# GroupNorm on one core: per-engine programs with hand-set semaphores, loops on TensorE and VectorE, all channels scaled on VectorE, 64 KB store rows

## The chip, the cores and the metric

The kernel runs on one core of one Trainium2 chip. The metric is the device time of one execution in microseconds. The kernel before takes 633.61 us (median of 3 runs, 633.52 to 633.78).

A core has five engines that run their own instruction streams: TensorE (PE), VectorE (DVE), ScalarE (ACT), GpSimd (POOL) and SyncE (SP), which issues the DMAs here. Sixteen DMA engines move data between HBM and the on-chip memory SBUF, whose 128 partitions are the rows that all engines work on; TensorE writes its results to PSUM.

## The reference

A GroupNorm over `x` of shape (128, 1024, 32, 16) in bf16: 128 samples, 32 groups of 32 channels, 512 pixels per channel. For each sample and group the mean and the variance are taken over 32 x 512 = 16384 elements.

```python
xr = x.reshape(B, G, C // G, H, W)
mu = xr.mean(axis=(2, 3, 4), keepdims=True)
var = ((xr - mu) ** 2).mean(axis=(2, 3, 4), keepdims=True)
xn = (xr - mu) / jnp.sqrt(var + 1e-5)
xn = xn.reshape(B, C, H, W)
return xn * g[None, :, None, None] + b[None, :, None, None]
```

The input is 134.2 MB and the output as large, so 268.4 MB pass the DMA engines.

## The kernel before

The work is cut into 32 tiles of 128 partitions. A partition holds one group of one sample: 32 channels of 512 elements, 32 KB in bf16, so a tile is 4 MB; here a tile `i` is called a unit. In tile `i` the partitions are 4 samples by 32 groups, and the 4 MB lie in one piece in HBM. Six tiles `xt` fit into SBUF at a time (`XBUFS`), and everything happens in place in them.

For each unit, in this order:

- `L(i)` (line 101) loads it through SP's queue; the first and the last unit are loaded in quarters, the others in one DMA of 4 MB.
- `M(i)` (line 166) sums over the free dimension: 32 matmuls with the identity `eye` as weights add the 32 slices of 512 columns into one PSUM tile `pa`. Each matmul has its own weight load.
- `R0(i)` (line 189): VectorE multiplies the PSUM tile by -1/16384 and accumulates it into `negmean`.
- `Q(i)` (line 244): ScalarE computes Square(x + negmean) over each half of the unit (128 x 8192) and accumulates the sum.
- `V(i)` (lines 308 to 353): ScalarE takes the square root of the variance, VectorE the reciprocal `rstd`, GpSimd the 32 factors per channel `scl`, `shift` and `bia`.
- `A(i)` (lines 363 and 368): each channel is scaled by `x * scl + bia`. Of the 32 channels VectorE does 16, GpSimd 13 and ScalarE 3.
- `S(i)` (line 381): the unit is stored, the last two units in quarters.

The main loop starts the sum of unit i+1 (`M`, `R0`) ahead of `V(i)` and `A(i)`, and `finish(i-1)`, which holds ScalarE's three channels, the store and the next loads, stands inside `Q(i)` between the two squares. The loads after the first six are issued in pairs, when two units have been stored; a load waits on SP until the store of the unit that had the buffer has landed. A tile framework writes the semaphores; `chain` only fixes the order of instructions on each engine. Units 0 and 31 are `shifted`: their squares are taken around the mean of their first quarter.

Of the kernel before, what the change touches and what calls it, by code (L numbers as in the profile page):

```python
# [9 lines left out]
ALU = mybir.AluOpType  # L10
F32 = mybir.dt.float32
# [6 lines left out]
XBUFS = 6  # L18
UPFRONT = 6
RUN = 2  # L20
MM_FREE = 512
QUARTERS = 4
STORE_IN_PARTS = 2
ACT_SHARE = 2
LAST_SHARE = 3
POOL_SHARE = 13
# [3 lines left out]
def kernel(  # L30
# [7 lines left out]

# [5 lines left out]
    assert P % G == 0 and C % G == 0  # L49
    NS = P // G  # L50
    assert B0 % NS == 0
    NT = B0 // NS
# [3 lines left out]
    MMN = MM_FREE  # L56
    NMM = F // MMN
    NQ = QUARTERS
    QF = F // NQ
    KQ = KC // NQ  # L60
    MQ = NMM // NQ
    assert NQ == 4 and F % (NQ * MMN) == 0 and KC % NQ == 0

    x_v = x.rearrange("(t n) (g k) h w -> t (n g) (k h w)", n=NS, g=G)
    o_v = out.rearrange("(t n) (g k) h w -> t (n g) (k h w)", n=NS, g=G)
    g_v = g.rearrange("(g k) -> g k", g=G)
    b_v = b.rearrange("(g k) -> g k", g=G)

    consts = ctx.enter_context(tc.tile_pool(name="consts", bufs=1))
    xpool = ctx.enter_context(tc.tile_pool(name="xpool", bufs=XBUFS))  # L70
    jpool = ctx.enter_context(tc.tile_pool(name="jpool", bufs=1))
    spool = ctx.enter_context(tc.tile_pool(name="spool", bufs=4))
    pspool = ctx.enter_context(
        tc.tile_pool(name="pspool", bufs=2, space=bass.MemoryType.PSUM)
    )
    gpool = ctx.enter_context(
        tc.tile_pool(name="gpool", bufs=1, space=bass.MemoryType.PSUM)
    )

    last = {}  # L80
    nosync = mybir.DependencyInfo(
        mybir.DependencyClass.NoSync, mybir.DependencyReason.DATA
    )

    def chain(key, inst):
        prev = last.get(key)
        if prev is not None:
            tc.add_manual_dep(inst.ins, prev.ins.name, nosync, reason="pipeline order")
        last[key] = inst
        return inst  # L90

    state = {}

    def L(i):
        xt = xpool.tile([P, F], BF16, name="xt")
        parts = NQ if i == 0 or i >= NT - 1 else 1
        w = F // parts
        for c in range(parts):
            chain(
                "sp",  # L100
                nc.sync.dma_start(  # L101
                    out=xt[:, c * w : (c + 1) * w], in_=x_v[i][:, c * w : (c + 1) * w]
                ),
            )
        state[i] = {"xt": xt}

    for i in range(min(UPFRONT, NT)):
        L(i)

    gb_b = consts.tile([G, 2, KC], BF16)  # L110
    chain("act", nc.scalar.dma_start(out=gb_b[:, 0, :], in_=g_v))
    chain("act", nc.scalar.dma_start(out=gb_b[:, 1, :], in_=b_v))
    eps_t = consts.tile([P, 1], F32)
    nc.vector.memset(eps_t[:], EPS)
    warm = consts.tile([P, 1], F32)
    chain("act", nc.scalar.activation(out=warm[:], in_=eps_t[:], func=ACT.Sqrt))  # L116

    ones_b = consts.tile([P, P], BF16)
    nc.vector.memset(ones_b[:], 1.0)
    eye = consts.tile([P, P], BF16)  # L120
    nc.gpsimd.affine_select(
        out=eye[:],
        in_=ones_b[:],
        pattern=[[-1, P]],
        compare_op=ALU.is_equal,
        fill=0.0,
        base=0,
        channel_multiplier=1,
    )
    rep = consts.tile([G, P], BF16)  # L130
    nc.gpsimd.affine_select(
        out=rep[:].rearrange("q (n a) -> q n a", n=NS),
        in_=ones_b[0:G, :].rearrange("q (n a) -> q n a", n=NS),
        pattern=[[0, NS], [-1, G]],
        compare_op=ALU.is_equal,
        fill=0.0,
        base=0,
        channel_multiplier=1,
    )
    gb = consts.tile([P, 2, KC], F32)  # L140
    gam = gb[:, 0, :]
    bet = gb[:, 1, :]

    def GB():
        gb_p = gpool.tile([P, 2, KC], F32, name="gb_p")
        chain(
            "pe",
            nc.tensor.matmul(  # L148
                out=gb_p[:].rearrange("p a k -> p (a k)"),
                lhsT=rep[:],  # L150
                rhs=gb_b[:].rearrange("q a k -> q (a k)"),
                start=True,
                stop=True,
            ),
        )
        chain("dve", nc.vector.tensor_copy(out=gb[:], in_=gb_p[:]))  # L156

    def shifted(i):
        return i == 0 or i == NT - 1

    def matmuls(st, name, lo, hi):
        ps = pspool.tile([P, MMN], F32, name=name)
        for k in range(lo, hi):
            chain(
                "pe",
                nc.tensor.matmul(  # L166
                    out=ps[:],
                    lhsT=eye[:],
                    rhs=st["xt"][:, k * MMN : (k + 1) * MMN],
                    start=(k == lo),  # L170
                    stop=(k == hi - 1),
                ),
            )
        st[name] = ps

    def M(i):
        st = state[i]
        if shifted(i):
            matmuls(st, "pa", 0, MQ)
            matmuls(st, "pb", MQ, NMM)  # L180
        else:
            matmuls(st, "pa", 0, NMM)

    def sum_of(ps, seed, name):
        total = spool.tile([P, 1], F32, name=name)
        jd = jpool.tile([P, MMN], BF16, name="jd")
        chain(
            "dve",
            nc.vector.tensor_scalar(  # L189
                out=jd[:],  # L190
                in0=ps[:],
                scalar1=-inv_n,
                scalar2=seed,
                op0=ALU.mult,
                op1=ALU.add,
                accum_out=total[:],
            ),
        )
        return total

    def R0(i):
        st = state[i]
        if shifted(i):
            st["q"] = sum_of(st["pa"], None, "q")
        else:
            st["negmean"] = sum_of(st["pa"], None, "negmean")

    def R1(i):
        st = state[i]
        if not shifted(i):  # L210
            return
        st["negmean"] = sum_of(st["pb"], st["q"][:], "negmean")
        off = spool.tile([P, 1], F32, name="off")
        chain(
            "pool",
            nc.gpsimd.tensor_scalar(  # L216
                out=off[:],
                in0=st["negmean"][:],
                scalar1=1.0 / NQ,
                scalar2=st["q"][:],  # L220
                op0=ALU.mult,
                op1=ALU.subtract,
            ),
        )
        seed = spool.tile([P, 1], F32, name="seed")
        chain(
            "pool",
            nc.gpsimd.tensor_scalar(
                out=seed[:],
                in0=off[:],  # L230
                scalar1=-1.0,
                scalar2=off[:],
                op0=ALU.mult,
                op1=ALU.mult,
            ),
        )
        st["seed"] = seed

    def squares(st, w, k, bias, scale, sq):

        ja = jpool.tile([P, F // 2], FP8, name="ja")
        chain(
            "act",
            nc.scalar.activation(  # L244
                out=ja[:, 0:w],
                in_=st["xt"][:, k * w : (k + 1) * w],
                func=ACT.Square,
                bias=bias,
                scale=scale,
                accum_out=sq,  # L250
                saturate=False,
            ),
        )

    def Q(i):

        st = state[i]
        if shifted(i):
            sq = spool.tile([P, NQ], F32, name="sq")
            for k in range(NQ):  # L260
                squares(st, QF, k, st["q"][:], 1.0 / NQ, sq[:, k : k + 1])
                if k == 0:
                    finish(i - 1)
            st["sq"] = sq
            return
        s0 = spool.tile([P, 1], F32, name="s0")
        s1 = spool.tile([P, 1], F32, name="s1")
        squares(st, F // 2, 0, st["negmean"][:], 1.0, s0[:])
        v0 = spool.tile([P, 1], F32, name="v0")
        finish(i - 1)  # L270
        chain(
            "pool",
            nc.gpsimd.tensor_scalar(  # L273
                out=v0[:],
                in0=s0[:],
                scalar1=inv_n,
                scalar2=EPS,
                op0=ALU.mult,
                op1=ALU.add,
            ),  # L280
        )
        squares(st, F // 2, 1, st["negmean"][:], 1.0, s1[:])
        st["v0"], st["s1"] = v0, s1
# [177 lines left out]
```

## Time and profile before

| what | value |
|---|---|
| device time, median of 3 runs | 633.61 us |
| the profiled execution: span of the profile | 632.5 us |
| DMA: share of the span that the data queue q1 kept 16 engines busy | 99.0% |
| HBM traffic over the span | 424 GB/s |
| busy: PE, DVE, ACT, POOL | 260.9, 379.0, 537.9, 345.3 us |
| squares on ACT, each 128 x 8192 | 7109 ns, 60 of them |
| scaling one channel: DVE, POOL, ACT (means) | 730, 801, 799 ns |
| one matmul of 128 x 512 (mean) | 421 ns |

The profile is of one execution, whose span lies 1.1 us below the median of the runs; its own device time is not listed, so 632.5 + 1.1 us is used for it. The page gives busy times per engine, a strip of 40 slices of the span, the DMA queues and groups of instructions by line; a timeline lists instructions with their start and duration; a list of waits says who waited for whom.

### The profile page before, as it was taken

The page shows a single profiled execution, that of the slowest core. Times are in us where ns is not written, and L with a number is a line of the kernel's source. Part 1 is how long each engine was busy: PE and PEld are TensorE (multiplying, and loading weights), DVE is VectorE, ACT ScalarE, POOL GpSimd, SP SyncE. Part 2 cuts the span into 40 slices and gives each one's busy share as a digit, 9 for nine tenths or more (in the row PEclk, how much of TensorE's full clock was granted, in tenths as well). Part 3 has the DMA queues.
Part 4 walks back from the last instruction along what each step waited for, and adds up shares of the span by engine and source line. Part 5 has one row for each costly group of instructions (what it writes and reads, how often), then busy time and mean ns, then how long its engine had stood idle before and what let it go on. Part 6 is the DMA issues. An engine that isn't in the chain of part 4 may idle for free.

```text
span 632.5 us, 3907 instructions
## 1 busy us (share of the span) xinstructions
PE 260.9 (41%) x1025; PEld 106.4 (17%) x1025; DVE 379.0 (60%) x645; ACT 537.9 (85%) x268; POOL 345.3 (55%) x523
## 2 busy tenths in 40 slices
PE   5577609064180632806327063270723607146000
PEld 2223203021030210302113021030301203012000
DVE  1077766666676477563665636666466663657660
ACT  4599999999999699696996969969798796987960
POOL 0077776666666377563665636666365663657100
PEclk9789759668595675957759577595875958758555
DMA  9999999999999999999999999999999999999996
GB/s 371 437 428 406 436 433 431 433 429 433 429 424 433 429 437 431 432 434 433 434 432 424 432 433 431 429 432 432 431 431 431 436 429 432 431 425 435 431 423 260
DMA packets 11063, 268.70 MB, mean 425 GB/s; under 512 B 1312, under 2 KB 1312, under 8 KB 1312
## 3 DMA queue, kind: packets, MB, share of 16 engines
q1 hardware_dynamic: 10944, 268.44, 99.0%
q8 instruction: 8, 0.13, 0.1%
q14 instruction: 15, 0.12, 0.0%
q10 hardware_dynamic: 96, 0.00, 0.0%
HBM read 134.22 MB, written 134.22 MB: 424 GB/s over the span
## 4 chain that ended last, share of the span: by engine, by line
DMA 62%; ACT 15%; PE 9%; issue 5%; DVE 3%; POOL 2%; SPq 0%; DVEq 0%; ACTq 0%; POOLq 0%
DMA out_dram<-xt 40%; DMA xt<-in_x_dram 21%; ACT ja L244 13%; PE pa L166 9%; DVE xt L368 3%; ACT xt L363 2%; POOL xt L368 1%; DMA gb_b<-in_g_dram 0%; ACT rstd L308 0%; POOL scl L337 0%; POOL shift L343 0%; POOL bia L353 0%; SPq L101 0%; DVE rstd L312 0%; DVE jd L189 0%
## 5 line engine op out<-in xcount | busy, mean ns | idle before, releaser
L244 ACT ACTIVATE ja<-xt,negmean 128x8192 fp8e5<-128x8192 bf16 x60 | 426.6, 7109 | 55.2 <-DVE jd L189 55.1
L166 PE MATMUL pa<-xt,eye 128*128 128x512 bf16 x976 | 250.1, 421 | 317.9 <-DMA xt<-in_x_dram 317.9
L368 DVE TENSOR_SCALAR xt<-xt,scl,bia 128x512 bf16<-128x512 bf16 x536 | 351.4, 730 | 39.8 <-POOL bia L353 39.8
L368 POOL TENSOR_SCALAR xt<-xt,scl,bia 128x512 bf16<-128x512 bf16 x390 | 307.5, 801 | 3.4 <-POOL bia L353 0.3
L166 PEld LDWEIGHTS <-eye 128*128 128x128 bf16 x1024 | 106.3, 106 | 472.2 <-DMA xt<-in_x_dram 318.8
L337 POOL TENSOR_SCALAR scl<-gb,rstd 128x32 f32<-128x32 f32 x31 | 11.1, 358 | 220.1 <-DVE rstd L312 220.1
L189 DVE TENSOR_SCALAR_CACHE_REDUCE jd<-pa 128x512 bf16<-128x512 f32 x32 | 21.9, 684 | 113.9 <-PE pa L166 113.9
L363 ACT ACTIVATE xt<-xt,bia,scl 128x512 bf16<-128x512 bf16 x98 | 72.0, 799 | 0.8 <-DVE bia L324 0.8
L312 DVE RECIPROCAL rstd<-rstd 128x1 f32<-128x1 f32 x32 | 5.2, 163 | 72.7 <-ACT rstd L308 72.7
L244 ACT ACTIVATE ja<-xt,q 128x4096 fp8e5<-128x4096 bf16 x8 | 29.7, 3706 | 6.6 <-DVE jd L189 6.4
L343 POOL TENSOR_SCALAR shift<-scl,negmean 128x32 f32<-128x32 f32 x31 | 11.1, 358 | 3.1
L216 POOL TENSOR_SCALAR off<-negmean,q 128x1 f32<-128x1 f32 x2 | 0.9, 430 | 20.4 <-DVE jd L189 20.4
L166 PE MATMUL pb<-xt,eye 128*128 128x512 bf16 x48 | 11.0, 379 | 0.6 <-DMA xt<-in_x_dram 0.6
L244 ACT ACTIVATION_READ_ACCUMULATOR ja<-xt,negmean 128x1 f32 x60 | 11.2, 187 | 0.0
L308 ACT ACTIVATE rstd<-s,v 128x1 f32<-128x1 f32 x30 | 8.8, 294 | 2.8
L353 POOL TENSOR_TENSOR bia<-shift,gb 128x32 f32<-128x32 f32 x31 | 7.8, 251 | 2.6
L273 POOL TENSOR_SCALAR v<-s 128x1 f32<-128x1 f32 x30 | 5.7, 191 | 2.5
L308 ACT ACTIVATE rstd<-var,eps_t 128x1 f32<-128x1 f32 x2 | 0.6, 294 | 7.5 <-DVE jv L292 7.5
L156 DVE COPY gb<-gb_p 128x64 f32<-128x64 f32 x1 | 0.2, 225 | 5.5 <-PE gb_p L148 5.5
L116 ACT ACT_TABLE_LOAD x1 | 1.3, 1283 | 1.7 <-PEq L445 1.7
L189 DVE DVE_READ_ACCUMULATOR jd<-pa 128x1 f32 x32 | 2.6, 80 | 0.0
L292 DVE TENSOR_SCALAR_CACHE_REDUCE jv<-sq,seed 128x4 f32<-128x4 f32 x2 | 0.4, 214 | 2.7 <-ACT ja L244 2.7
(18 smaller groups left out, 6.1 us busy)
## 6 DMA issues: line engine op xcount, KB each, us to landing
xt<-in_x_dram SPq DMA_DIRECT2D x30, 4096.0 KB, 19.4
out_dram<-xt SPq DMA_DIRECT2D x30, 4096.0 KB, 29.3
xt<-in_x_dram SPq DMA_DIRECT2D x8, 1024.0 KB, 11.5
out_dram<-xt SPq DMA_DIRECT2D x8, 1024.0 KB, 17.9
gb_b<-in_g_dram ACTq DMA_DIRECT2D x1, 2.0 KB, 3.2
gb_b<-in_b_dram ACTq DMA_DIRECT2D x1, 2.0 KB, 5.2
```

The source lines that it names most:

```text
L116: chain("act", nc.scalar.activation(out=warm[:], in_=eps_t[:], func=ACT.Sqrt))
L166: nc.tensor.matmul(out=ps[:], lhsT=eye[:], rhs=st["xt"][:, k * MMN : (k + 1) * MMN], start=(k == lo), stop=(k == hi - 1),),
L189: nc.vector.tensor_scalar(out=jd[:], in0=ps[:], scalar1=-inv_n, scalar2=seed, op0=ALU.mult, op1=ALU.add, accum_out=total[:],),
L244: nc.scalar.activation(out=ja[:, 0:w], in_=st["xt"][:, k * w : (k + 1) * w], func=ACT.Square, bias=bias, scale=scale, accum_out=sq, satura ...
L273: nc.gpsimd.tensor_scalar(out=v0[:], in0=s0[:], scalar1=inv_n, scalar2=EPS, op0=ALU.mult, op1=ALU.add,),
L308: nc.scalar.activation(out=rstd[:], in_=last_sum[:], func=ACT.Sqrt, bias=bias[:], scale=scale),
L312: chain("dve", nc.vector.reciprocal(out=rstd[:], in_=rstd[:]))
L337: nc.gpsimd.tensor_scalar(out=scl[:], in0=gam, scalar1=rstd[:], scalar2=None, op0=ALU.mult),
L343: nc.gpsimd.tensor_scalar(out=shift[:], in0=scl[:], scalar1=st["negmean"][:], scalar2=None, op0=ALU.mult,),
L353: nc.gpsimd.tensor_tensor(out=bia[:], in0=shift[:], in1=bet, op=ALU.add),
L363: inst = nc.scalar.activation(out=span, in_=span, func=ACT.Identity, bias=bia, scale=scl)
L368: inst = eng.tensor_scalar(out=span, in0=span, scalar1=scl, scalar2=bia, op0=ALU.mult, op1=ALU.add,)
```

## The change

The work per element is the same. What differs:

- **Layout.** A partition row in HBM is now 64 KB: two neighbouring groups of one sample. 8 samples by 16 pairs of groups make 128 rows, and each of the 32 units is one half (32 KB) of all rows, so that a unit's load takes 32 KB out of every 64 KB. The six buffers lie side by side in one tensor `ring`, so that two neighbouring units can be stored as one DMA of 128 rows of 64 KB (8 MB).
- **Order of DMAs.** All on SP, written by hand: six loads; then units 0 to 5 stored one by one with loads between; units 6 to 29 stored in 12 pairs, each pair followed by two loads; unit 30 alone; unit 31 in four parts. In the steady part the first of the two loads needs the pair stored before, the second one the pair just issued.
- **TensorE** loads the identity once and issues the matmuls without a weight load; a loop of 5 rounds with 6 units in each.
- **ScalarE** does the squares, one small ACTIVATE that forms `part`, and the root; no channels. Each of its steps waits for its own step before.
- **VectorE** loops over 31 units: reciprocal, `scl`, `bia`, the mean of the next unit, then all 32 channels of this one. Addresses and semaphore counts are computed in registers: in the built program a register instruction stands ahead of each of the 32 scaling instructions, and register instructions with waits stand between the small steps. The last unit is written out without a loop.
- **GpSimd** makes two constants at the start and does nothing after.
- `negmean`, `sq`, `std`, `scl` and `bia` exist once, not in four buffers.
- The root is taken for every unit in the same way; units 0 and 31 are no longer `shifted`, and unit 0 is loaded in one piece.

The core of the new code (constants: `SLOTS = 6`, `PAIR = 2`, `SKEW = 2`, `DONE = 30`):

```python
+    x_v = x.rearrange("(t n) (q k) h w -> t (n q) (k h w)", n=NS, q=GQ)   # GQ = 16, NS = 8
+    ring = sb("xt", [P, SLOTS * F], BF16)
...
+    def sync_program(sp):
...
+        for u in range(SLOTS):
+            load(sp, u)
+        for u in range(SLOTS):
+            sp.wait_ge(scaled, u + 1)
+            keep(u, 1)
+            if u == PAIR - 1:
+                fill(SLOTS)
+                fill(SLOTS + 1)
+            elif u > PAIR:
+                fill(SLOTS + u - 1)
+        for u in range(SLOTS, DONE, PAIR):
+            sp.wait_ge(scaled, u + PAIR)
+            keep(u, PAIR)
+            fill(u + SLOTS - SKEW + 1)
+            fill(u + SLOTS - SKEW + 2)
+        sp.wait_ge(scaled, DONE + 1)
+        store(sp, DONE, 1)
+        w = F // LAST_PARTS
+        for c in range(LAST_PARTS):
+            sp.wait_ge(scaled, DONE + 2 + c)
+            store(sp, DONE + 1, 1, c * w, (c + 1) * w)
...
+        with nc.Fori(0, TRIPS, head_slot={ET.PE: 0}, engines=[ET.PE]) as r:
+            for j in range(SLOTS):
+                s = (j + PAIR) % SLOTS
+                pe.wait_ge(ld[s], r * 16 + (16 if j + PAIR < SLOTS else 32))
+                pe.wait_ge(means, r * SLOTS + (j + 1))
+                add_up(pe, s)
...
+    def spread(act, u):
+        act.wait_ge(means, u + 1)
+        for h in range(HALVES):
+            lo = (u % SLOTS) * F + h * (F // HALVES)
+            if h:
+                act.wait_ge(squared, 3 * u + h)
+            act.activation(out=junk[:], in_=ring[:, lo : lo + F // HALVES], func=ACT.Square,
+                           bias=negmean[:], scale=1.0, accum_out=sq[:, h : h + 1],
+                           saturate=False).then_inc(squared, 1)
...
+        with nc.Fori(0, NT - 1, head_slot={ET.DVE: 0}, engines=[ET.DVE]) as u:
+            half = v.snap((u % PAIR) * KC)
+            bank = v.snap(MM_FREE - (u % PAIR) * MM_FREE)
+            v.wait_ge(rooted, u + 1)
+            factors(v, gb[:, 0, bass.ds(half, KC)], gb[:, 1, bass.ds(half, KC)], u * 3 + 2)
+            v.wait_ge(summed, u + 2)
+            mean_of(v, ps_flat[:, bass.ds(bank, MM_FREE)])
+            for k in range(KC):
+                at = v.snap((u % SLOTS) * F + k * HW)
+                inst = scale(v, k, ring[:, bass.ds(at, HW)])
+            inst.then_inc(scaled, 1)
```

`keep` stores units and notes the count that their landing will show; `fill(u)` waits for the landing of the store of unit u-6 and then loads unit u; `factors` is reciprocal, `scl` and `bia` with a wait for VectorE's own semaphore `own` after each.

## The prediction

> **What bounds the kernel now.** First the page: how full the DMA engines are, and which engines work beside them.
>
> ```profile
> span 632.5 us, 3907 instructions
> PE 260.9 (41%) x1025; PEld 106.4 (17%) x1025; DVE 379.0 (60%) x645; ACT 537.9 (85%) x268; POOL 345.3 (55%) x523
> DMA  9999999999999999999999999999999999999996
> q1 hardware_dynamic: 10944, 268.44, 99.0%
> q8 instruction: 8, 0.13, 0.1%
> q14 instruction: 15, 0.12, 0.0%
> ```
>
> The DMA strip is at nine tenths or more from the first slice to the last but one, and the data queue alone takes 99% of 16 engines: the kernel runs at the pace of its transfers, and ScalarE at 85% is next. q8 and q14 are the engines' own code, fetched on the same 16 DMA engines (columns: packets, MB, share). Then the list of waits of SP's queue:
>
> ```profile
> SPq L101 <- DMA out_dram<-xt: 453.2, 26, 29.0
> SPq L381 <- DVE xt L368: 124.0, 14, 37.0
> ```
>
> SP waits most for stores to land before it may load again, with work queued ahead of it. Then the timeline, for one unit's period on ScalarE and for VectorE with and without GpSimd beside it (start, duration):
>
> ```profile
> 149.46 7.11 ACT L244 ACTIVATE ja<-xt,negmean 128x8192 fp8e5<-128x8192 bf16 x1
> 156.48 0.19 ACT L244 ACTIVATION_READ_ACCUMULATOR ja<-xt,negmean 128x1 f32 x1
> 165.97 0.29 ACT L308 ACTIVATE rstd<-s,v 128x1 f32<-128x1 f32 x1
> 166.18 7.11 ACT L244 ACTIVATE ja<-xt,negmean 128x8192 fp8e5<-128x8192 bf16 x1
> 572.58 0.69 DVE L189 TENSOR_SCALAR_CACHE_REDUCE jd<-pa 128x512 bf16<-128x512 f32 x1 [9.72 <-PE pa L166]
> 573.20 0.08 DVE L189 DVE_READ_ACCUMULATOR jd<-pa 128x1 f32 x1
> 573.20 0.16 DVE L312 RECIPROCAL rstd<-rstd 128x1 f32<-128x1 f32 x1
> 574.64 11.11 DVE L368 TENSOR_SCALAR xt<-xt,scl,bia 128x512 bf16<-128x512 bf16 x16 [1.28 <-POOL bia L353]
> 591.62 5.26 DVE L368 TENSOR_SCALAR xt<-xt,scl,bia 128x512 bf16<-128x512 bf16 x16 [1.28 <-POOL bia L353]
> 606.24 0.24 DVE L318 TENSOR_SCALAR scl<-gb,rstd 128x32 f32<-128x32 f32 x1
> 606.51 0.25 DVE L324 SCALAR_TENSOR_TENSOR bia<-scl,negmean,gb 128x32 f32<-128x32 f32 x1
> ```
>
> A unit takes ScalarE 16.72 us (149.46 to 166.18), while two transfers of 4 MB take 19.4 us: compute is 2.7 us per unit faster than the DMA. Sixteen channels cost VectorE 11.11 us beside GpSimd's scaling, 5.26 us without it: 0.694 and 0.329 us each.
>
> The trace's DMA packets, counted one by one: a 32 KB row takes 1213 ns (median), an 8 KB row 309. A DMA of 4 MB gives each engine 8 rows and ends 9.68 us after the one before. First packets start at 1.8 to 2.4 us. The 17th unit moved is done at 168.2 us on the first DMA engine and 171.0 on the last, the very last DMA at 625.5 and 631.2: some engines fall 5.7 us behind, in jumps of 0.3 to 1.2 us, many at the times of the code fetches.
>
> **Part by part.** Own time of this execution: 632.5 us of span, 633.6 with the 1.1 us around it.
>
> *Row sizes.* Two packet sizes give (1213-309)/24576 = 0.0368 ns per byte and 7.7 ns per packet. A 64 KB row is then 2418 ns instead of 2 x 1213: 12 pair stores x 8 rows per engine x 8 ns = 0.8 us saved; between nothing (if a row is cut in two) and this. Twelve fewer quartered DMAs: 96 rows of 8 KB (29.7 us) become 24 of 32 KB (29.1): 0.5 us. Together -1.3 us. The loads' 64 KB pitch costs nothing: the quartered loads now have 8 KB rows at 32 KB pitch and take the same 309 ns.
>
> *Code.* TensorE's 2052 listed instructions become some 270 with a loop, VectorE's 645 some 130. The 23 fetches (8 of 16 KB, 15 of 8 KB) mostly go, and with them about half of the lag of the slowest DMA engine: -2.5 us, between 0 and -5. [...]
>
> *Held weights, and channels off GpSimd and ScalarE.* TensorE (7.08 to 9.8 us per unit, of 19.4) was never late; its weight loads were hidden, so their end is worth nothing. VectorE gets 32 channels per unit: 32 x 0.329 = 10.5 us with GpSimd silent, under ScalarE's 15 us. This holds if each register instruction hides under the channel before it. No such instruction is in the trace; bounds per instruction are 0.04 us (the gap from a mean's end, 573.28, to the square that waits for it, 573.32) and 0.34 (SP's issue of a load in the chain of waits). A register instruction resembles an issue, but does less: I take 0.17, which hides; at 0.34 a unit's scaling becomes 10.9 us.
>
> *The chain per unit.* One `negmean` and one program order on VectorE now tie the engines in a ring: mean(u), squares, root, factors(u), mean(u+1). Before, the mean of the next unit was ready ahead, and ScalarE went from root to square without a wait. ScalarE: 2 x 7.21 (149.46 to 156.67) + 2 x 0.29 + four hops of 0.04 = 15.2. VectorE: 0.16 + 0.24 + 0.25 + 0.70 = 1.35, hops 0.2, and six register instructions with waits among them, 6 x 0.17 = 1.0 (0 to 2.0). A = 17.7 us per unit, between 16.7 and 18.7. [...]
>
> 17.7 is still under 19.4, so the steady part stays with the DMA. A pair store must be ready when the two loads ahead of it end; the odd unit's load has landed some 48 us before that, and mean, A and scaling after it take about 39: some 8 us to spare. The two ends are where it shows:
>
> *Start.* Unit 0 arrives whole at about 12.7 us instead of by quarters from 5.5. The sum takes 8.43 us (as unit 1's now, from 22.72), the mean 0.7: mean(0) is done at 21.9. From there the ring turns without rest. The first pair store needs units 6 and 7, so it moves at 21.9 + 8A + 10.5 + 1.4 (from issue to first packet, as at the start) = 33.8 + 8 x 17.7 = 175.4 us. Before it only 17 unit transfers are queued (six loads, six stores, five loads), because SP issues the store ahead of the next load: the queue is empty at 168.2 to 171.0, less about 1 us of the last for the fetches. The gap is about 5.5 us on the slowest engine; it is zero up to A = 17.0.
>
> *End.* Unit 30's channels stand behind mean(31), and nothing is left to load. From the last load's end to the first packet of store 30: landing 0.6, sum 8.4 to 9.8, mean 0.7, scaling 10.5, issue 1.4 = 21.6 to 23.0 us, with one pair store of 19.4 to cover it: a gap of 2.2 to 3.6, I take 3.0.
>
> *Closing.* Two more barriers of the block: +0.5 us (0 to 1).
>
> Sum: 175.4 + 47 transfers x 9.683 = 455.1, -1.2 rows, +1.6 lag collected after the gap, +3.0 at the end = 633.9 for the last packet; +1.3 to the end of the span as now (631.2 to 632.5), +1.1 around it, +0.5: 636.8 us, +0.5%. About 0.2%, 1.3 us, is what a measurement of this kernel can tell from no change.
>
> **Rivals.**
>
> *The ring is short enough* (A at most 17.0: register instructions near the 0.04 bound). Then the queue never empties at the start, and fewer fetches and small rows show: 169.7 + 455.1 - 1.2 + 1.4 + 2.3 + 2.4 = 629.7, up to 632.3 with less of the lag gone. For it: all rows that the trace does show are that short, and A has only to lose 0.7. Against: three waits of VectorE on itself with addresses computed behind them. This is the faster side; 22%.
>
> *It balances*: A about 17.2, a gap of 1.5 us at the start and the 3.0 at the end against 3.8 us saved: 632.3 to 634.9, no change. 14%.
>
> *VectorE becomes the bound.* If register instruction and issue together take over 0.53 us per channel, 32 of them and 2.5 us for the rest pass 19.4 us per unit; from there VectorE sets the pace: at 0.6 us, 22 + 32 x 21.7 = 716 us. Against: it is over one and a half times SP's issue of a DMA. 8%. Should VectorE keep its present 0.694 us with GpSimd idle it would be still slower; the row at 591.62 excludes it.
>
> My forecast, slower by the two gaps (634.9 to about 648, the upper end with A = 18.7 and 10.9 us of scaling: 33.8 + 149.6 + 0.4 = 183.8 for the pair store, 645 at the end, and 3 more if the lag stays): 56%.
>
> **How the numbers follow.** Slower 56 + 8 = 64%, same 14, faster 22. The range 630.5 to 648 leaves out the lowest tenth and the case of VectorE as the bound. The likeliest case alone: 635 to 645.
>
> **What would show it.** Right: a dip in the DMA strip near 170 us (slice 11) and one near 600, DMA full between; ScalarE's unit period about 17.7 us in the first 170 us; VectorE's channels at 0.33 us; q8 nearly gone; SP waiting for VectorE at the first pair store. Wrong: channels spaced wider than 0.35 us, DMA holes in the steady part, a period under 17, or 64 KB rows at another rate than 2.42 us.

## The result and the profile after

The changed kernel takes 640.97 us (median of 4 runs, 640.21 to 641.19) against 633.62 us: a ratio of 1.0114, 95% interval 1.0099 to 1.0128. The direction was the one forecast and the time lies within the range on record; the size, 1.14%, is well above the 0.5% on record. The profiled execution took 640.92 us, 2.1 us more than its span.

The page of the changed kernel (span; busy time by engine; the DMA strip and GB/s in 40 slices of 16 us; the DMA queues as packets, MB, share):

```profile
span 638.8 us, 3963 instructions
PE 265.5 (42%) x1025; PEld 0.2 (0%) x2; DVE 374.9 (59%) x1187; ACT 482.1 (75%) x194; POOL 0.8 (0%) x6
DMA  8999999999899999999999999999999999999968
GB/s 361 439 441 394 427 437 439 435 427 429 369 394 427 427 398 456 417 435 453 408 453 410 433 453 414 447 414 443 443 417 445 414 443 421 435 445 404 404 295 361
q1 hardware_dynamic: 7920, 268.44, 98.0%
q14 instruction: 4, 0.03, 0.0%
q8 instruction: 1, 0.02, 0.0%
```

Weight loads are gone (2 for 1025) and code fetches nearly so (q8 from 8 to 1, q14 from 15 to 4), GpSimd is silent (0.8 us busy for 345.3). VectorE, with twice the channels, is no busier (374.9 us for 379.0): a channel takes half as long, 0.326 us (10.43 us for 32) for 0.694 beside GpSimd. The DMA strip has the two dips that were forecast, slice 11 (160 to 176 us, 369 GB/s) and slice 39 (295 GB/s). One more is unforeseen: slice 12, after the first dip, has only 394 GB/s. Single slices are to be read with care: the page counts a packet where it starts, so sixteen packets of 32 KB more or less are 33 GB/s. Times "by the packets" below are therefore counted from the trace's DMA packets, each spread over the time it takes. The DMA queue's own waits:

```profile
SPq L101 <- DMA out_dram<-xt: 320.9, 15, 30.7
SPq L109 <- DVE xt L272: 288.9, 23, 46.3
```

SP's wait for VectorE before a store (124.0 us before, line 381) is now nearly as long as its wait for stores to land. The timeline of one turn of the ring, and of the issue of the first pair store (start, duration, idle time before it):

```profile
40.08 7.12 ACT L209 ACTIVATE ja<-xt,negmean 128x8192 fp8e5<-128x8192 bf16 x1 [2.25 <-DVE jd L244]
54.90 0.29 ACT L227 ACTIVATE std<-sq,part 128x1 f32<-128x1 f32 x1
55.23 0.16 DVE L255 RECIPROCAL rstd<-std 128x1 f32<-128x1 f32 x1 [4.84 <-ACT std L227]
55.60 0.24 DVE L257 TENSOR_SCALAR scl<-gb,rstd 128x32 f32 x1 [0.20 <-DVE rstd L255]
55.98 0.25 DVE L261 SCALAR_TENSOR_TENSOR bia<-scl,negmean,gb 128x32 f32<-128x32 f32 x1
56.66 0.69 DVE L244 TENSOR_SCALAR_CACHE_REDUCE jd<-ps 128x512 bf16 x1 [0.43 <-DVE bia L261]
57.28 10.43 DVE L272 TENSOR_SCALAR xt<-xt,scl,bia  x32
57.40 7.12 ACT L209 ACTIVATE ja<-xt,negmean 128x8192 fp8e5<-128x8192 bf16 x1 [2.20 <-DVE jd L244]
171.60 0.33 SPq L109 DMA_DIRECT2D out_dram<-xt  x1
```

The ring turns in 17.32 us (40.08 to 57.40; 17.7 on record) and 32 channels take 10.43 (10.5). The pair store is issued at 171.60, and by the packets it moves from 172.5 on (172.44 to 172.58 on the sixteen engines); the 17 transfers ahead of it were done at 168.3 us on the first DMA engine and 171.7 on the last. So the last engine stood idle for 0.8 us, and the sixteen for 3.5 us on average, because fourteen of them were done early.

### The profile page after: what moved, and what is told of

It reads as the page before. It is cut to its first block, busy times and chain, and to the rows that moved or that the text cites. A ratio compares the mean times of both kernels' runs of the same rounds, so it can differ in the third digit from the quotient of the medians.

```text
span 638.8 us, 3963 instructions
## 1 busy us (share of the span) xinstructions
PE 265.5 (42%) x1025; PEld 0.2 (0%) x2; DVE 374.9 (59%) x1187; ACT 482.1 (75%) x194; POOL 0.8 (0%) x6
## 4 chain that ended last, share of the span: by engine, by line
DMA 38%; ACT 33%; PE 10%; DVE 10%; issue 5%; DVEq 2%; SPq 0%
DMA xt<-in_x_dram 38%; ACT ja L209 32%; PE ps L156 10%; DVE xt L272 8%; DVEq L272 1%; DVE jd L244 1%; ACT part L219 1%; ACT std L227 1%; DVE bia L261 1%; DVE scl L257 1%; DVEq L244 0%; DVE rstd L255 0%; SPq L109 0%; DVEq L257 0%; DVEq L261 0%
## 5 line engine op out<-in xcount | busy, mean ns | idle before, releaser
L209 ACT ACTIVATE ja<-xt,negmean 128x8192 fp8e5<-128x8192 bf16 x64 | 455.8, 7122 | 134.9 <-DVE jd L244 133.9
L156 PE MATMUL ps<-xt,eye 128*128 128x512 bf16 x1024 | 265.3, 425 | 330.8 <-DMA xt<-in_x_dram 308.8
L272 DVE TENSOR_SCALAR xt<-xt,scl,bia (+1 forms) x1024 | 333.5, 409 | 0.0
L255 DVE RECIPROCAL rstd<-std 128x1 f32<-128x1 f32 x32 | 5.3, 164 | 165.3 <-ACT std L227 165.3
L244 DVE TENSOR_SCALAR_CACHE_REDUCE jd<-ps 128x512 bf16 (+1 forms) x32 | 22.1, 692 | 72.6 <-PE ps L156 64.0
L257 DVE TENSOR_SCALAR scl<-gb,rstd 128x32 f32 (+1 forms) x32 | 7.7, 241 | 6.4 <-DVE rstd L255 6.4
L261 DVE SCALAR_TENSOR_TENSOR bia<-scl,negmean,gb 128x32 f32<-128x32 f32 x32 | 8.1, 252 | 4.5 <-DVE scl L257 0.2
L227 ACT ACTIVATE std<-sq,part 128x1 f32<-128x1 f32 x32 | 9.4, 294 | 1.0
L219 ACT ACTIVATE part<-sq,eps_t 128x1 f32<-128x1 f32 x32 | 9.4, 294 | 1.0
L192 PEld LDWEIGHTS <-eye 128*128 128x128 bf16 x1 | 0.1, 102 | 0.1
```

The costliest lines, as they stand in the source:

```text
L156: return pe.add_instruction(mybir.InstMatmult(name=nc.get_next_instruction_name(), engine=ET.PE, ins=[pe.lower_ap(rhs), pe.lower_ap(eye[:] ...
L209: act.activation(out=junk[:], in_=ring[:, lo : lo + F // HALVES], func=ACT.Square, bias=negmean[:], scale=1.0, accum_out=sq[:, h : h + 1], ...
L219: act.activation(out=part[:], in_=sq[:, 0:1], func=ACT.Identity, bias=eps_t[:], scale=inv_n,).then_inc(squared, 1)
L227: act.activation(out=std[:], in_=sq[:, 1:2], func=ACT.Sqrt, bias=part[:], scale=inv_n,).then_inc(rooted, 1)
L244: v.tensor_scalar(out=jd[:], in0=sums, scalar1=-inv_n, scalar2=None, op0=ALU.mult, op1=ALU.add, accum_out=negmean[:],).then_inc(means, 1)
L255: v.reciprocal(out=rstd[:], in_=std[:]).then_inc(own, 1)
```

## The experiments

All times are set against the kernel before, run on the same chip beside them; runs are compared with each other by these ratios, since the medians come from two chips. Where an expectation below has the pair store of the changed kernel move at 173.0 us and its gap at 1.3 us, the packets say 172.5 and 0.8.

**The load of unit 11 ahead of the first pair store.**

```diff
+            if u == SLOTS:
+                fill(u + SLOTS - SKEW + 1)
             sp.wait_ge(scaled, u + PAIR)
             keep(u, PAIR)
-            fill(u + SLOTS - SKEW + 1)
+            if u > SLOTS:
+                fill(u + SLOTS - SKEW + 1)
             fill(u + SLOTS - SKEW + 2)
```

> Edit: the load of unit 11 is issued before the store of units 6 and 7 instead of after it, so that 18 units of transfers are queued ahead of that store and not 17. In the changed kernel the queue is empty from 168.3 us (first DMA engine done) or 171.7 (last) to 173.0. Theory 1 (the time is that of the slowest DMA engine, and an engine's delays stay with it): 1.3 us are won, 640.97 -> 639.7. Theory 2 (the empty queue costs what the first engines lose, because after it all engines stand level and pay anew for their delays, such as the 1 us that all sixteen lose together at 209 to 211 us): up to 4.7 us, 636.3. In both the trace shows no dip of the DMA strip near 170 us.

Measured: 1.0125 (1.0109 to 1.0140), 641.86 us: nothing won. The GB/s of its page, and SP's next load in its timeline:

```profile
GB/s 361 446 433 393 432 442 434 428 427 432 442 436 303 422 397 459 406 438 455 401 455 410 432 457 406 459 410 438 451 406 447 420 444 422 433 444 399 342 360 361
```

```profile
201.03 0.33 SPq L101 DMA_DIRECT2D xt<-in_x_dram  x1
```

Slice 11 is full (442), slice 13 has the hole (303). The pair store ends at 197.3 to 200.7 us, and the next load, which waits for its landing, is issued at 201.03 with nothing queued. The hole was moved, not closed, and neither theory was tested.

**The load of unit 31 directly behind that of unit 30.**

```diff
             keep(u, PAIR)
-            fill(u + SLOTS - SKEW + 1)
+            if u + SLOTS - SKEW + 1 < NT - 1:
+                fill(u + SLOTS - SKEW + 1)
             fill(u + SLOTS - SKEW + 2)
+            if u + SLOTS - SKEW + 2 == NT - PAIR:
+                fill(NT - 1)
```

> Edit: the load of unit 31 is issued directly after that of unit 30, ahead of the store of units 26 and 27 (its buffer is free by then). In the changed kernel 42.3 us of work of unit 31 (landing 594.5 to the last packet at 636.9) stand against 38.7 us of transfers behind its load. Theory (the end is unit 31's chain: sum, squares, root, 32 channels in turn): it gets 19.4 us of cover more, the DMA queue stays full to the end, 3.2 to 3.6 us are won, 640.97 -> 637.6. Rival (the end is set by the DMA engines that have fallen behind, 4.3 us by then): the last engine has as many packets left as before, under 1 us is won, 640.

Measured: 1.0063 (1.0049 to 1.0077), 638.20 us: 0.51% or 3.2 us won, the amount of the theory; its place is another. What stood at the end, in the timeline of the changed kernel:

```profile
595.11 9.64 PE L156 MATMUL ps<-xt,eye 128*128 128x512 bf16 x32 [22.31 <-DMA xt<-in_x_dram]
605.10 0.69 DVE L244 TENSOR_SCALAR_CACHE_REDUCE jd<-ps 128x512 bf16 x1 [5.80 <-PE ps L156]
605.71 10.42 DVE L272 TENSOR_SCALAR xt<-xt,scl,bia  x32
605.83 7.12 ACT L209 ACTIVATE ja<-xt,negmean 128x8192 fp8e5<-128x8192 bf16 x1 [7.58 <-DVE jd L244]
621.75 10.43 DVE L272 TENSOR_SCALAR xt<-xt,scl,bia 128x512 bf16<-128x512 bf16 x32
```

TensorE waits 22 us for unit 31, its sum ends at 605, its mean follows at 605.10, and only then come the channels of unit 30 (605.71 to 616.1) and at last those of unit 31 (621.75 to 632.2). By the packets all engines are idle from 614.1 to 617.0 us, until the store of unit 30 moves, and then full to the last packet at 636.9: what was lost stood in front of unit 30's store, and with the load moved up that store follows the one before without a gap.

**Both together.** 

> Both reorderings of the queue together. If the gaps at the start and at the end are separate losses, the sum of the two alone: 640.97 - 1.3 - 3.4 = 636.3 by theory 1, 633 by theory 2. What is then left over the kernel before (633.6) is delays of the DMA engines and the barriers at the end (the last packet is followed by 4.0 us now, 2.4 before).

Measured: 1.0088 (1.0074 to 1.0102), 639.71 us: the end's gain less what the moved hole costs.

**Loops written out.** `for r in range(TRIPS)` and `for u in range(NT - 1)` in place of the two hardware loops, constant addresses and counts.

> Edit: the loops of TensorE and VectorE are written out; addresses and semaphore counts are constants; weights stay held. Code is fetched again (the before kernel fetched 23 pieces, the changed one 4 in the measured stretch). Theory of the record (code fetches make the DMA engines fall behind): some 10 fetches come back, and the last engine falls 1.5 to 3 us further behind the first than 4.3 us. Rival (the engines fall behind at the switch from loads to stores, whatever is fetched): the spread stays at 4 to 5 us. In both the register instructions go from the ring (gaps of 0.20, 0.17 and 0.43 us between VectorE's small steps become 0.04): unit period 17.3 -> 16.7 us, the first pair store moves 4.8 us earlier and its gap closes. Time: 640.5 by the first, 638 to 639.7 by the second.

Measured: 1.0119 (1.0103 to 1.0134), 641.12 us: no gain. Its small steps on VectorE in the timeline, and the code queues on its page:

```profile
55.62 0.16 DVE L255 RECIPROCAL rstd<-std 128x1 f32<-128x1 f32 x1 [4.85 <-ACT std L227]
55.82 0.24 DVE L257 TENSOR_SCALAR scl<-gb,rstd 128x32 f32<-128x32 f32 x1
56.09 0.25 DVE L261 SCALAR_TENSOR_TENSOR bia<-scl,negmean,gb 128x32 f32<-128x32 f32 x1
56.38 0.69 DVE L244 TENSOR_SCALAR_CACHE_REDUCE jd<-ps 128x512 bf16<-128x512 f32 x1
```

```profile
q8 instruction: 4, 0.07, 0.0%
q14 instruction: 12, 0.10, 0.0%
```

The steps now follow each other within 0.04 us and the ring turns in 16.64 us (squares at 40.47 and 57.11), so the register instructions cost 0.68 us per unit. The first pair store moves 4.3 us earlier (issued at 167.30), yet the last engine ends the load of unit 31 at 594.4 us against 594.5. With 11 fetches more its spread (first to last DMA engine at that load) is 7.3 us instead of 4.3. That looks like the 3 us of the fetch theory, but it isn't: in the changed kernel the hole had set all engines level (0.6 us apart at 193), here they start 3.5 us apart (at 188 to 192). From there to the load of unit 31 the spread grows by 3.8 us here and by 3.7 in the changed kernel. Here six jumps of the last engine, 0.7 to 1.0 us each, lie in transfers during which 8 KB of code were fetched; with the loops it loses as much with a single fetch in that time. And closing the hole gained nothing here, although the first engine stood idle for 0.06 us only and the last not at all: all engines still lost 0.6 us between 185 and 191 and 0.8 between 205 and 209.

**Units 6 to 11 stored singly**, on top of the moved load of unit 31: `range(2 * SLOTS)` for the single stores, pairs from unit 12.

> Base: the run with the load of unit 31 moved up (1.0063 of before, 638.2 us). Edit: units 6 to 11 are stored one by one as well, each followed by one load; pairs begin with unit 12. In the first reordering of the start the hole only moved (a load that waits for the pair's landing stood alone behind it); here two transfers are always queued while the ring works, and unit 6 is stored 17 us before unit 7 is ready, so the queue never runs empty at the start. Theory 1 (slowest engine): 1.3 us won. Theory 2 (the first engine's loss counts, and the second stall of all engines near 210 us comes from their standing level after the hole): 4 to 5 us won, 633.5. Rival: the hole does not matter at all, the engines fall behind as much more, 638.

Measured: 0.9999 (0.9990 to 1.0008), 633.50 us: 0.64% or 4.1 us under its base. The size is that of theory 2, and theory 1 and the rival fall; that the second stall comes from the engines' standing level is not shown by it. Its page:

```profile
GB/s 366 429 432 409 432 432 434 436 430 434 434 434 434 432 430 430 432 432 463 401 463 403 455 426 421 446 419 448 432 428 436 428 436 436 424 455 413 349 403 336
```

Slices 11 to 15, which were 369, 394, 427, 427 and 398 in the changed kernel, are 434, 434, 434, 432 and 430: not only the dip has gone, but what followed it. By the packets (means of the sixteen engines) 0.9 to 1.3 us are lost between 56 and 66 us in every kernel here, the one before included. Where a hole stood at 168 to 173 us, 0.8 to 0.9 are lost again between 187 and 195 and 1.0 to 1.1 between 207 and 214. In this run these last two are below 0.1. Another hole is left near the end: the pair store of units 28 and 29 waits for unit 29, and from 584.2 us on the engines run empty one by one until it moves at about 590; the last engine is just done then.

**All units stored singly** up to unit 29, on the same base.

> As the run before it, but all units 0 to 29 are stored one by one with one load behind each: stores and loads alternate every 9.7 us (some 50 switches) where pairs switch every 19.4 (some 25). The rows of the stores are 32 KB. If the DMA engines fall behind at the switches from loads to stores, the last engine is 8 us behind the first by the end instead of 4.3, and the time is 3 to 4 us over the run with pairs from unit 12. If they fall behind at a rate per byte or by code fetches, nothing changes but the 0.7 us of the longer rows. The cover of a unit's chain grows from 48 to 77 us of transfers, which by the profile is not needed.

Measured: 0.9997 (0.9988 to 1.0006), 633.90 us; spread 5.7 us at the store of unit 29, against 6.0 with pairs from unit 12. Twice the switches and the same spread at the end: a lag of fixed size per switch is excluded. The switches themselves are not, for the packets show where the spread grows. From the eighth transfer on, 2.2 of 2.5 us come in the 25 loads that have a store behind them, and almost none (0.05) in the 24 stores that have a load behind them; from 310 to 560 us the spread stays at 5.3 through 13 more such loads. It grows at changes from loads to stores, and then stops growing. The hole near 590 us of the run before is absent here, and the time is the same (0.9997 and 0.9999): there it cost nothing that can be measured.

**Pairs as two DMAs with 32 KB rows**, on the base with unit 31's load moved: `keep(u, 1)` and `keep(u + 1, 1)` for `keep(u, PAIR)`.

> Base: the run with the load of unit 31 moved up (1.0063). Edit: each pair is stored by two DMAs of 128 rows of 32 KB instead of one with rows of 64 KB, issued one behind the other at the same place. By packet times (2 x 1213 against 2418 ns, 12 stores x 8 rows per engine) 0.8 us slower, 639.0. Rival (the second load now waits for the first half's store only and is issued 9.7 us earlier, so more is queued): 0.5 us or more faster; or no difference.

Measured: 1.0090 (1.0077 to 1.0103), 639.71 us: 0.27% slower, 1.7 us where 0.8 was expected. No run here says where the rest comes from.

**Without the frame of the tile framework**, same base: the block of programs directly on the core, no `tile_critical` and no context around it.

> Base: the run with the load of unit 31 moved up (1.0063). Edit: the per-engine programs run without the tile framework's frame around them, so that its barriers before and after the block go. The changed kernel has 1.9 us from the last packet to the end of the span and 2.1 us around the span, before has 1.3 and 1.1. If these barriers are that 1.6 us: 638.2 -> 636.6. If the block's own barriers, which stay, are: 638.

Measured: 1.0050 (1.0037 to 1.0064), 636.96 us: 0.13% less, the intervals overlap. The next two give it a second and a third time.

**Three repairs together** (no change but those above).

> Units 0 to 11 stored one by one, the load of unit 31 moved up, and no frame of the tile framework: the three repairs together. If they add up: 0.9999 - 0.0013 = 0.9986 of before, 633.1 us, the first version under it by a hair. If the frame's time was hidden or belonged to that kernel: 1.000.

Measured: 0.9985 (0.9976 to 0.9994), 632.71 us.

**All units stored singly, without the frame.**

> All units stored one by one, and no frame. Sum of the single results: 0.9997 - 0.0013 = 0.9984, 633.0 us. With the run before it this also weighs 64 KB rows against 32 KB rows without a hole in the queue: by packet times pairs are ahead by 0.6 us; the singles so far were equal.

Measured: 0.9975 (0.9965 to 0.9985), 632.13 us: under both kernels, by 0.25% and 1.4%. The frame is worth 0.13, 0.14 and 0.22% in three pairs; the last packet is followed by 2.0 us of span with it (629.4 to 631.4) and 0.8 without (628.5 to 629.3). Single stores with 32 KB rows are not slower than pairs with 64 KB rows (0.9975 for 0.9985), so the 1.7 us of the two DMAs per pair are no price of the row size as such (the run with pairs still has its hole near 590 us, so this is no clean comparison of rows).

**Transfers alone.** Each store waits only for its load (`sp.wait_ge(ld[s], ...)` for `scaled`); no other engine has a program; the output is x.

> Only the transfers: order and sizes of the kernel with the load of unit 31 moved up, each store waiting only for its load to land; nothing is computed, the output is x. The queue is never empty. If the engines fall behind each other because of what the compute engines do or fetch, the spread at the end is under 1 us and the first stall of all sixteen near 58 us may go too: last packet at about 623, time 627. If it is the transfers' own: spread 5 to 6 us, time 632 to 633.

> As the run of transfers alone, but the store of units 6 and 7 waits until all 17 transfers before it have landed: one hole of some 2 to 3 us on the slowest engine near 172 us, all engines level after it. Theory: the hole costs itself and a second stall of all engines about 36 us later (1 us), and the spread is collected anew: 3.5 to 5 us over the run without it. Rival (a hole costs what the last engine stands idle): 2 to 3 us, no second stall.

The second run's edit:

```diff
+            if u == SLOTS:
+                sp.wait_ge(st[SLOTS - 1], sent[SLOTS - 1])
+                for j in range(SLOTS, 2 * SLOTS - 1):
+                    landed(j)
             landed(u)
             landed(u + 1)
             keep(u, PAIR)
```

Measured: 0.9961 (0.9946 to 0.9976), 631.35 us without the hole, and 1.0025 (1.0015 to 1.0035), 635.28 us with it. The lines of their pages, the queue that never empties first:

```profile
GB/s 366 433 433 403 435 435 435 435 430 435 445 420 433 441 418 447 420 433 449 416 449 408 439 426 424 433 414 449 430 422 447 422 453 426 424 437 457 412 419 284
q14 instruction: 1, 0.01, 0.0%
```

```profile
GB/s 365 431 433 420 435 433 433 431 431 429 400 398 431 431 398 464 398 431 431 431 431 416 443 449 420 429 420 439 454 418 447 412 447 437 414 429 445 423 423 319
```

The hole lies in slice 11 (400 GB/s against 445). By the packets the sixteen engines stood idle for 2.1 us on average (the last one for about 1.5, done at 169.2 and moving again at 170.7), and they lost 0.9 near 187 to 193 and 1.0 near 207 to 212; without the hole 0.0 and 0.3 are lost at these two places. The medians are 3.9 us apart, the two profiled executions 2.5: with the hole the engines are 2.1 us apart at the end and not 4.0, which gives back a part. So by the medians a hole in this stream costs about twice its mean length, with no compute engine at work.

The run without the hole has one code fetch on its page (q14: 1) and by the packets none during its transfers, and still a spread of 4.0 us from 400 us on. That spread needs neither fetches nor compute. From the eighth transfer on all of its growth, 3.1 us, comes in loads with a store behind them.

The two losses after a hole lie at changes of direction too: at the end of the pair store, with a load behind it, and at the end of the two loads that follow, with a store behind them. They don't keep a fixed distance from the restart. With the load of unit 11 moved up, a load restarts the queue at 202 us; all engines lose 1.4 us at 210 to 213, where the next store begins, and nothing near 218 or 238. Near 590 us, with units 6 to 11 stored singly, a store restarts it and a store follows: under 0.2 us is lost up to 620. Why these changes cost all engines something after a hole and little elsewhere, and why single engines lag at them, stays open; no run here separates it.

## Why the prediction was right in direction and wrong in size

| term of the sum | on record | measured | difference |
|---|---|---|---|
| first packet of the first pair store | 175.4 | 172.5 | -2.9 |
| from there to the end of the load of unit 31, last engine (43 transfers) | 416.8 | 422.0 | +5.2 |
| from there to the last packet (38.7 of transfers and a gap) | 41.7 | 42.4 | +0.7 |
| last packet to device time | 2.9 | 4.0 | +1.1 |
| sum | 636.8 | 640.9 | +4.1 |

*Right.* The DMA stays the bound in the steady part (the strip at nine tenths or more in slices 12 to 38); VectorE at 0.326 us per channel without GpSimd; register instructions hidden under the channels (10.43 us for 32 with them, 10.42 with the loops written out); the ring of mean, squares, root and factors, and the two places where it shows. All three rivals fall: the ring is not short enough, it does not balance, VectorE is not the bound.

*The step that failed* is the lag that follows the gap in the sum ("+1.6 lag collected after the gap"). It halved the old lag of the slowest DMA engine because the fetches go ("Code"), and took the stream behind the gap for an undisturbed one. Against the pace of the packets (9.681 us for 4 MB, 19.319 for a pair) the last engine lost 6.2 us between the hole and the end of unit 31's load: 2.0 in two stalls of all engines, and some 4 in its own lag (spread 0.6 us at 193, 4.3 at 594). Where the queue did not run empty at the start (units 6 to 11 stored singly) it lost 2.6 over as many transfers, not far from the 1.6. And in the transfers alone, with no fetch, a hole was enough to cost 3.9. So what the record left out is what a hole brings after it.

How much of the old lag the fetches make stays open. With one fetch in the stretch and no hole at the start the last engine lost 2.1 to 2.6 us over 43 transfers, in the kernel before 4.0 over 39 with 15 fetches; but 3.5 with none at all, in the transfers alone.

*The price of the gap* failed with it. The record let a gap cost what the slowest engine stands idle, 5.5 us. By that measure it was 0.8 us (1.2 in the run with the load of unit 31 moved), since the pair store came earlier than forecast; removing it brought 4.1. The two errors, a gap taken too long and a lag taken too small, have opposite signs; that they partly cancel is luck.

*The ring's length*: 17.32 for 17.7. Six register instructions were put at 0.17 us each; they cost 0.68 together, 0.11 each. The loops run on few code fetches: five in the whole span (q8 1, q14 4, against 8 and 15 before), and in the trace none starts between those at 138.2 and 546.7 us.

*The end* was right in size and mechanism: unit 30's store waits behind mean(31), and all engines are idle from 614.1 to 617.0 us, 2.9 for 3.0; the 38.7 us of transfers took 39.5. Unit 31's own channels end at 632.2, its last quarter begins to move at 634.4 when the quarters before it are through, so its chain was close behind but did not bind. Moving one load up closed the gap.

*Rows*: packet times are as worked out (a 64 KB row takes 2418 ns). What they are worth in time isn't settled: 1.7 us in one pair of runs, nothing in another.

*Closing*: +1.6 us over before, for the author's estimate of 0.5; the frame is about 1 us of it (0.8 to 1.4 in the three pairs).

Against the 1.14% stand the end with 0.51%, the start's hole with what it drags along with 0.64%, and the frame with 0.14%; without the three the design is at 0.9985 with pairs and 0.9975 with single stores, the latter 0.8 us above the run of transfers alone (which has pairs and the frame).

## What to carry to other kernels

When a kernel runs at the pace of a full DMA queue, look for the first moment at which the queue can run empty: count the transfers queued ahead of each wait, and the compute that must finish in that time. Price such a hole by a run of the transfers alone with and without it, not by its length; in these runs a hole at the start cost more than the last engine's idle time (3.9 us for 1.5 in the transfers alone), and one near the end, for which the last engine did not wait, nothing that could be measured (0.9999 with it, 0.9997 without). At the end, set the chain of the last unit against the transfers behind its load, and move that load up before shortening the chain. A coincidence in time (here jumps at code fetches) is a suspicion until a run has the one without the other; and an equal value at the end clears no suspect, as long as one hasn't looked where it grows.

## What the runs showed of the hardware

- A hole of 2.1 us (mean of 16 DMA engines; 1.5 on the last) in a stream of 4 MB and 8 MB transfers cost 3.9 us by the medians. All engines lost 0.9 and 1.0 us more, at the next two changes between stores and loads. An idle queue isn't needed for it: with the loops written out it was empty for 0.06 us on one engine at most, and 0.6 and 0.8 us were lost at the same two changes.
- Sixteen engines with equal packets drift apart by 4.0 us in 400 us with no code fetch and no compute, all of it from the eighth transfer on in loads that have a store behind them; after that the spread stays. In whole kernels with five fetches, and a queue that does not run empty at the start, it reaches 5.4 to 6.0.
- VectorE's two-scalar multiply-add on 128 x 512 bf16 takes 0.326 us with GpSimd silent, 0.694 beside its scaling; an address computed in a register ahead of each costs nothing there (32 channels: 10.43 us with it, 10.42 with constant addresses).
